# The forward products of decays in a linear-attention kernel: reciprocals of the backward products in place of a second scan

## The chip, the cores and the metric

The kernel runs on one core of a Trainium2 chip. The metric is the device time of one launch in microseconds (us); three runs of the kernel before the change gave 976.2, 979.26 and 980.47 us, a median of 979.26. The engines of the core are TensorE (PE; its weight loads are PEld), VectorE (DVE), ScalarE (ACT), GpSimd (POOL) and SyncE (SP), which issues most of the loads and stores. Each engine works through its own list of instructions in a fixed order and waits on semaphores for the others.

## The reference

Three layers follow each other; the change lies in the first, a recurrence over 768 positions with a state of 40 x 40 for each of 4 batches and 8 heads:

```python
for t in range(S):
    kt, vt, rt = (k[:, :, t], v[:, :, t], r[:, :, t])
    wt, at, bt = (w[:, :, t], a[:, :, t], b[:, :, t])
    y[:, :, t] = np.einsum('bhd,bhde->bhe', rt, state)
    Sa = np.einsum('bhde,bhe->bhd', state, at)
    state_decay = state * wt[:, :, None, :] - np.einsum('bhd,bhe->bhde', Sa, bt)
    state = state_decay + np.einsum('bhd,bhe->bhde', vt, kt)
```

All of it is in fp32. The decays `w` lie between 0.85 and 0.95. The second layer is a gated block (a product, a convolution of three taps, a sigmoid gate, a product), the third adds a two-dimensional Fourier transform, normalizes and runs a two-layer block.

## The kernel before

The recurrence is done in 12 chunks of 64 positions. Within a chunk the effect of the decays is taken out by scaling: `a` is multiplied, and `k` and `b` are divided, by products of decays, so that the rest is made of plain products on TensorE and the inverse of a triangular matrix for each head. A chunk is handled in two halves of two batches, so there are 24 halves, and for each of them `decay` (L153) runs once. Its tiles have 120 partitions (three heads of 40) and six rows of 66 columns: 64 positions with a column of padding at each end. The padding of `w` is zero and that of `ends` is one (column 0 and column 65), so that one scan over 396 columns restarts in each of the six rows.

In `decay`, the first scan (L161) runs backward and gives `vx`: in column 1 + j stands the product of the decays from position j to the end of the chunk. `kb` is multiplied by it on GpSimd (L176). Then a reciprocal of the six entries of column 1 goes into column 0 of `ends` (L164), and a second scan (L165) runs forward from it and gives `wx`: in column j the reciprocal of the product from position j to the end. `a` is multiplied by `wx` (L168; on VectorE in the first chunk, on GpSimd in all others), and goes as a block-diagonal tile `abd` to the products `gram` (L219): by L172 in the first chunk, by three DMAs issued by SP (L175) in the others. `squares` (L247, ScalarE) sums the squares of `wx` and `vx` for a check of the range. Column 65 of `wx` gets a copy of column 1 of `vx` (L166, GpSimd), with which `stage_s` (L458) scales the state; `stage_o` (L509) multiplies the outputs by `wx`.

The order: `run` (L594) writes the first chunks out by hand (with `half`, L632), and then loops over 52 steps, one for each batch of each chunk and a tail of four. A step interleaves the stages of the recurrence, the decays and grams of later chunks (`ahead`, L578: the decay of half (n + 18) / 2 at step n), the inverse of the next group of chunks (L308; many small products on VectorE, L275 and L278 in the first two groups, L333 and L336 in the others), and pieces of preparation for the weights of the later layers (L778 to L785, L752). On top of this a scheduler orders the instructions of each engine when the kernel is built, by its own estimates; TensorE's order is kept as written. `vx` has two buffers, `wx` twelve, `w` and `kb` three. Before the first loads arrive, four products on `ends` (L599) warm TensorE up.

The lines on which all turns:

```python
nc.vector.reciprocal(self.ends.rearrange("p (a b) -> p a b", b=66)[:, :, 0:1], vx[:, :, 1:2])
nc.vector.tensor_tensor_scan(flat[1], flat[0], self.ends, 0.0, op0=ALU.mult, op1=ALU.add)
nc.gpsimd.tensor_copy(wx[:, :, 65:66], vx[:, :, 1:2])
```

Of the kernel before, what the change touches and what calls it, by code (L numbers as in the profile page):

```python
# [15 lines left out]
ALU = mybir.AluOpType  # L16
# [4 lines left out]
C = 64  # L21
# [77 lines left out]
class Attn:  # L99
# [53 lines left out]
    def decay(self, c, hb):  # L153
        nc, pre = self.nc, self.pre
        d = self.hf[c, hb]
        w, a, kb = d["w"], d["a"], d["kb"]

        wx = pre.tile([P3, 6, 66], F32, name="wx", tag="wx", bufs=12)
        vx = self.early.tile([P3, 6, 66], F32, name="vx", tag="vx", bufs=2)
        flat = [v.rearrange("p a b -> p (a b)") for v in (w, wx, vx)]  # L160
        nc.vector.tensor_tensor_scan(flat[2][:, ::-1], flat[0][:, ::-1], self.ends[:, ::-1], 0.0,  # L161
                                     op0=ALU.mult, op1=ALU.add)

        nc.vector.reciprocal(self.ends.rearrange("p (a b) -> p a b", b=66)[:, :, 0:1], vx[:, :, 1:2])  # L164
        nc.vector.tensor_tensor_scan(flat[1], flat[0], self.ends, 0.0, op0=ALU.mult, op1=ALU.add)  # L165
        nc.gpsimd.tensor_copy(wx[:, :, 65:66], vx[:, :, 1:2])  # L166
        e = nc.vector if c < 1 else nc.gpsimd
        e.tensor_tensor(a, a, wx[:, :, 0:C], op=ALU.mult)  # L168
        for h in range(HG):
            if c < 1:  # L170
                mul = nc.vector.tensor_scalar_mul if h == 2 else nc.scalar.mul
                v = mul(self.abd[hb][:, h], a, self.mdiag[:, D * h:D * h + 1])  # L172
                self.late = self.late if h == 2 else v
            else:
                nc.sync.dma_start(self.abd[hb][D * h:D * h + D, h], a[D * h:D * h + D])  # L175
        self.markp = nc.gpsimd.tensor_tensor(kb, kb, vx[:, :, 2:66].unsqueeze(2).to_broadcast([P3, 6, 2, C]), op=ALU.mult)  # L176
        d.update(wx=wx, vx=vx)
# [1232 lines left out]
```

## Time and profile before

| | |
|---|---|
| median of 3 runs | 979.26 us |
| profiled execution | 977.45 us |
| its span | 975.5 us |
| PE busy | 818.7 us (84%) |
| DVE busy | 668.3 us (69%) |
| ACT busy | 519.7 us (53%) |
| POOL busy | 433.2 us (44%) |
| mean granted TensorE clock | 0.925 |

The span is the time from the first to the last instruction of the profiled execution. Busy time is the time in which an engine works on an instruction; waiting is not counted. The recurrence fills the first 480 us, the other two layers the rest. The 24 decays lie between 3.5 us and 341 us.

### The profile page before, as it was taken

To read this page: it belongs to the slowest core of one execution; us is meant where nothing else is said; L and a number is where in the kernel's file an instruction comes from. 1 tells how busy PE (TensorE), PEld (TensorE's weight loads), DVE (VectorE), ACT (ScalarE), POOL (GpSimd) and SP (SyncE) were. 2 spreads that over 40 slices of the span, in tenths; PEclk is the share of its full clock that TensorE was granted. 3 is DMA by queue.
4 is the path that set the end of the run, shared out by engine and by line. 5 is a ranking of instruction groups with operands and counts; after the bars stand their busy time and mean duration, and the time that the engine had idled before them with its cause. 6 is when DMAs were issued, how large, how long until landed. Compare 5 with 4: busy or idle time off the path is not lost. (4 is left out here: it accounts for less than half of the span.)

```text
span 975.5 us, 21804 instructions
## 1 busy us (share of the span) xinstructions
PE 818.7 (84%) x8178; PEld 745.1 (76%) x8178; DVE 668.3 (69%) x1320; ACT 519.7 (53%) x1448; POOL 433.2 (44%) x507
## 2 busy tenths in 40 slices
PE   5457765776886787877899899899999999999997
PEld 3446655676776787776877677777889999999997
DVE  6994897998997898942378688788773544424321
ACT  4747685577676785543566665656553321312211
POOL 5465355465565553532368557665662130101000
PEclk8758797898898999988999999999999999999999
DMA  9623262566564654539444643213004000000001
GB/s 231 187 57 108 80 172 72 167 172 164 162 175 109 172 138 114 159 101 262 121 123 111 208 122 92 79 29 94 14 26 151 22 1 21 21 21 22 21 14 32
DMA packets 102990, 101.16 MB, mean 104 GB/s; under 512 B 47272, under 2 KB 89115, under 8 KB 102875
## 3 DMA queue, kind: packets, MB, share of 16 engines
q1 hardware_dynamic: 100907, 94.73, 34.7%
q0 software_dynamic: 1968, 4.93, 1.7%
q8 instruction: 67, 1.10, 0.5%
q14 instruction: 48, 0.39, 0.1%
HBM read 74.81 MB, written 20.76 MB: 98 GB/s over the span
## 5 line engine op out<-in xcount | busy, mean ns | idle before, releaser
L1132 DVE SCALAR_TENSOR_TENSOR gl<-hp,gh 128x384 fp32r<-128x384 f32 x80 | 44.4, 556 | 111.3 <-ACT gh L1131 111.2
L895 PE MATMUL acc<-w_out_f,z 128*128 128x320 f32 x384 | 116.6, 441 | 3.6 <-POOL z L882 2.1
L1131 ACT ACTIVATE gh<-hp 128x384 fp32r<-128x384 f32 x80 | 39.3, 492 | 149.7 <-PE hp L701 149.6
L878 DVE SCALAR_TENSOR_TENSOR c<-h,cw,c 128x384 f32<-128x384 f32 x128 | 101.6, 798 | 17.3 <-ACT c L876 15.4
L895 PEld LDWEIGHTS acc<-w_out_f,z 128*128 128x128 f32 x384 | 72.1, 193 | 28.2 <-POOL z L882 3.9
L701 PE MATMUL hp<-xh,w_in_h 128*128 128x386 f32 x192 | 76.4, 398 | 12.1 <-ACT h L869 11.9
L701 PE MATMUL hp<-uh,w_ch_h 128*128 128x384 f32 x240 | 82.3, 343 | 0.0
L701 PE MATMUL hp<-ul,w_ch_h 128*128 128x384 f32 x240 | 81.0, 337 | 0.0
L388 PE MATMUL yp<-x,gt 128*64 128x40 f32 x768 | 64.9, 244 | 18.8 <-DVE gt L470 18.4
L1155 POOL DMA_INDIRECT out<-o,rows x12 | 11.8, 982 | 150.8 <-DVE o L1150 131.9
L388 PEld LDWEIGHTS yp<-x,gt 128*64 128x64 f32 x768 | 60.0, 148 | 21.4 <-DVE gt L470 21.4
L219 PE MATMUL gram<-abd,kb 120*128 120x192 f32 (+1 forms) x288 | 59.5, 353 | 17.8 <-DMA a<-in_a 11.2
L1145 PE MATMUL acc<-w_ch_h,gh 128*128 128x320 f32 x240 | 73.2, 312 | 0.0
L1145 PE MATMUL acc<-w_ch_l,gh 128*128 128x320 f32 x240 | 73.0, 309 | 0.0
L333 DVE TENSOR_TENSOR tmp<-A 128x30 f32<-128x30 f32 (+9 forms) x150 | 70.1, 467 | 3.1
L219 PEld LDWEIGHTS gram<-abd,kb 120*128 120x128 f32 x288 | 55.1, 224 | 19.4 <-issue 11.6
L336 DVE TENSOR_TENSOR A<-A,tmp 128x30 f32<-128x30 f32 (+9 forms) x150 | 67.3, 449 | 2.9
L701 PE MATMUL hp<-xl,w_in_h 128*128 128x386 f32 x192 | 67.4, 351 | 0.0
L388 PE MATMUL gp<-rbd,zt 120*128 120x192 f32 (+1 forms) x288 | 59.0, 347 | 7.1 <-ACT zt L437 4.0
L782 POOL TENSOR_TENSOR pm<-pm,py 128x160 int32<-128x160 int32 (+2 forms) x64 | 44.4, 693 | 41.2 <-DVE pm L780 22.3
L879 ACT ACTIVATE c<-c 128x384 f32<-128x384 f32 x64 | 33.4, 521 | 53.9 <-DVE c L878 53.5
L1145 PE MATMUL acc<-w_ch_h,gl 128*128 128x320 f32 x240 | 61.4, 309 | 0.0
(225 smaller groups left out, 2565.0 us busy)
## 6 DMA issues: line engine op xcount, KB each, us to landing
kb<-in_kb SPq DMA_DIRECT2D x24, 360.0 KB
vbd<-in_vbd SPq DMA_DIRECT2D x24, 320.0 KB
xd<-xo SPq DMA_DIRECT2D x56, 90.0 KB
w<-in_w SPq DMA_DIRECT2D x24, 185.6 KB
a<-in_a SPq DMA_DIRECT2D x24, 180.0 KB
z<-in_zv SPq DMA_DIRECT2D x24, 180.0 KB
zt<-in_vt SPq DMA_DIRECT2D x24, 180.0 KB
rbd<-in_r SPq DMA_DIRECT2D x72, 60.0 KB
```

What stands on the lines that cost most here:

```text
L219: nc.tensor.matmul(gp[:, 192 * gi:192 * gi + 64 * nh], d["kb"][:, bl * NG + gi].rearrange("p a b -> p (a b)"), abd[:, 0:nh, bl * NG + gi], ...
L333: nc.vector.tensor_tensor(tmp, A[:, s + 1:32, s:s + 1].to_broadcast([128, n, s]), A[:, s:s + 1, 0:s].to_broadcast([128, n, s]), op=ALU.mult)
L336: nc.vector.tensor_tensor(A[:, s + 1:32, 0:s], A[:, s + 1:32, 0:s], tmp, op=ALU.add)
L388: self.lastpe = op(*args, **kw)
L701: nc.tensor.matmul(out, l, r, start=(j == 0), stop=(j == len(ops) - 1))
L782: nc.gpsimd.tensor_tensor(m, m, y, op=ALU.add)
L878: nc.vector.scalar_tensor_tensor(c, h[:, j:HS + j], cw[:, f, j:j + 1], c, op0=ALU.mult, op1=ALU.add)
L879: nc.scalar.activation(c, c, AF.Sigmoid)
L895: nc.tensor.matmul(self.acc[t][:, 0:DM], z[:, ts], w[:, f], start=(f == 0), stop=(f == NF1 - 1))
L1131: self.mark = nc.scalar.activation(gh, hp[:, 0:HS], AF.Relu)
L1132: nc.vector.scalar_tensor_tensor(gl, hp[:, 0:HS], 0.0, gh.bitcast(F32), op0=ALU.max, op1=ALU.subtract)
L1145: nc.tensor.matmul(self.acc[t][:, 0:DM], l[:, ts], r, start=(f == 0 and j == 0), stop=(f == NF2 - 1 and j == 2))
```

## The change

The small reciprocal into `ends` and the forward scan are replaced by one reciprocal of 6 x 64 elements, from the backward products straight into `wx`. The value is the same product: column j of `wx` is one over column j + 1 of `vx`. Column 64 of `wx`, which the scan wrote and nothing reads, is no longer written. `ends` keeps its first contents.

```diff
-        nc.vector.reciprocal(self.ends.rearrange("p (a b) -> p a b", b=66)[:, :, 0:1], vx[:, :, 1:2])
-        nc.vector.tensor_tensor_scan(flat[1], flat[0], self.ends, 0.0, op0=ALU.mult, op1=ALU.add)
+        nc.vector.reciprocal(wx[:, :, 0:C], vx[:, :, 1:C + 1])
         nc.gpsimd.tensor_copy(wx[:, :, 65:66], vx[:, :, 1:2])
```

The changed kernel has one line less, so its lines behind L164 carry numbers lower by one. TensorE's order is the same in both. VectorE's order at the start of the program, before (a scan is named SCALAR_TENSOR_TENSOR here):

```order
L161 SCALAR_TENSOR_TENSOR vx<-w,ends 120x396
L164 RECIPROCAL ends<-vx 120x6
L165 SCALAR_TENSOR_TENSOR wx<-w,ends 120x396
L161 SCALAR_TENSOR_TENSOR vx<-w,ends 120x396
L168 TENSOR_TENSOR a<-a,wx 120x384
L164 RECIPROCAL ends<-vx 120x6
L172 TENSOR_SCALAR abd_89<-a,mdiag 120x384
L165 SCALAR_TENSOR_TENSOR wx<-w,ends 120x396
L168 TENSOR_TENSOR a<-a,wx 120x384
L172 TENSOR_SCALAR abd_90<-a,mdiag 120x384
```

And VectorE's order at the same place after:

```order
L161 SCALAR_TENSOR_TENSOR vx<-w,ends 120x396
L164 RECIPROCAL wx<-vx 120x6x64
L161 SCALAR_TENSOR_TENSOR vx<-w,ends 120x396
L167 TENSOR_TENSOR a<-a,wx 120x384
L164 RECIPROCAL wx<-vx 120x6x64
L171 TENSOR_SCALAR abd_89<-a,mdiag 120x384
L167 TENSOR_TENSOR a<-a,wx 120x384
L171 TENSOR_SCALAR abd_90<-a,mdiag 120x384
```

The wide reciprocal stands where the small one stood, and the second scan of each decay is gone from between the operations that feed the first grams.

VectorE's order between the two steps of the inverse of the first group, before (L286 gives TensorE the operands of the first products, L300 takes their result):

```order
L286 STREAM_TRANSPOSE t_479<-A 128x32x32
L161 SCALAR_TENSOR_TENSOR vx<-w,ends 120x396
L164 RECIPROCAL ends<-vx 120x6
L165 SCALAR_TENSOR_TENSOR wx<-w,ends 120x396
L161 SCALAR_TENSOR_TENSOR vx<-w,ends 120x396
L313 STREAM_TRANSPOSE A<-l_350 128x1024
L164 RECIPROCAL ends<-vx 120x6
L165 SCALAR_TENSOR_TENSOR wx<-w,ends 120x396
L161 SCALAR_TENSOR_TENSOR vx<-w,ends 120x396
L164 RECIPROCAL ends<-vx 120x6
L165 SCALAR_TENSOR_TENSOR wx<-w,ends 120x396
L270 MEMSET A 128x32
```

And after, at the same place (L299 is the former L300):

```order
L161 SCALAR_TENSOR_TENSOR vx<-w,ends 120x396 x2
L164 RECIPROCAL wx<-vx 120x6x64
L312 STREAM_TRANSPOSE A<-l_348 128x1024
L164 RECIPROCAL wx<-vx 120x6x64
L161 SCALAR_TENSOR_TENSOR vx<-w,ends 120x396
L269 MEMSET A 128x32
L274 TENSOR_TENSOR tmp<-A 128x28
L164 RECIPROCAL wx<-vx 120x6x64
L299 SCALAR_TENSOR_TENSOR t_475<-t_475,mlt,xd 128x16x16
```

Three decays stand ahead of L300 in both; after the change a first product of the next group's inverse stands there too, and the small reciprocals and scans are three wide reciprocals.

## Rows read from the trace of the kernel before

**Rows 1.** Busy time of each engine by stretch of the span; columns in the first line.
```profile
core 0: us, PE busy (x) PEld busy (x) DVE busy (x) ACT busy (x) POOL busy (x), PEclk, DMA share, GB/s
...
10.00:40.00 30.00, 15.26 (x96) 14.81 (x97) 25.60 (x57) 20.44 (x65) 14.44 (x15) 0.72 0.96 253
40.00:75.00 35.00, 17.03 (x437) 15.36 (x435) 33.86 (x55) 19.63 (x64) 19.09 (x20) 0.61 0.20 57
75.00:100.00 25.00, 19.54 (x403) 18.48 (x404) 10.96 (x16) 17.96 (x61) 13.77 (x16) 0.86 0.36 99
100.00:250.00 150.00, 105.04 (x1651) 96.92 (x1651) 133.60 (x263) 102.10 (x323) 79.82 (x85) 0.86 0.50 138
250.00:302.00 52.00, 41.34 (x499) 37.41 (x496) 51.20 (x104) 36.72 (x124) 33.85 (x40) 0.93 0.61 170
302.00:345.00 43.00, 33.19 (x571) 30.91 (x570) 33.81 (x79) 29.61 (x96) 21.80 (x26) 0.84 0.54 143
345.00:480.00 135.00, 111.34 (x1891) 101.74 (x1888) 84.76 (x200) 71.90 (x204) 50.99 (x65) 0.92 0.55 150
```

**Rows 2.** Lines L164, L165 and L1064: duration ns min/median/max, first and last start us.
```profile
L164 DVE RECIPROCAL ends<-vx x24: 160/186/195, 7.0 to 324.1; 120x6 f32<-120x6 f32 x24
...
L165 DVE TENSOR_TENSOR_SCAN wx<-w,ends x24: 968/1098/2389, 7.2 to 339.3; 120x396 f32<-120x396 f32 x24
...
L1064 DVE RECIPROCAL rs<-rs x4: 166/180/191, 707.1 to 883.0; 128x6 f32<-128x6 f32 x4
```

**Rows 3.** Groups of DVE instructions by shape: busy us, mean ns, idle before.
```profile
L165 DVE TENSOR_TENSOR_SCAN wx<-w,ends 120x396 f32<-120x396 f32 x24 | 31.4, 1310 | 0.3
...
L164 DVE RECIPROCAL ends<-vx 120x6 f32<-120x6 f32 x24 | 4.5, 186 | 2.8 <-PE warm L599 2.5
...
L760 DVE COPY cw<-pm 128x24 f32<-128x24 f32 x1 | 0.2, 177 | 0.0
```

**Rows 4.** DVE's timeline from 36 to 45 us: start us, duration us, instruction.
```profile
36.02 0.28 DVE L275 TENSOR_TENSOR tmp<-A 128x112 f32<-128x112 f32 x1
...
39.88 0.19 DVE L275 TENSOR_TENSOR tmp<-A 128x28 f32<-128x28 f32 x1
...
44.91 0.19 DVE L164 RECIPROCAL ends<-vx 120x6 f32<-120x6 f32 x1
```

**Rows 5.** DVE's timeline at the start, with the idle time before in brackets.
```profile
3.53 0.98 DVE L161 TENSOR_TENSOR_SCAN vx<-w,ends 120x396 f32<-120x396 f32 x1 [2.03 <-DMA w<-in_w]
7.01 0.19 DVE L164 RECIPROCAL ends<-vx 120x6 f32<-120x6 f32 x1 [2.49 <-PE warm L599]
```

**Rows 6.** Busy time of line L165 alone, by stretch: length, DVE busy, clock, DMA.
```profile
0.00:75.00 75.00, 13.81 (x9) 0.70 0.59 157
75.00:100.00 25.00, 3.18 (x3) 0.86 0.36 99
100.00:250.00 150.00, 7.87 (x6) 0.86 0.50 138
250.00:302.00 52.00, 4.11 (x4) 0.93 0.61 170
302.00:345.00 43.00, 2.47 (x2) 0.84 0.54 143
```

**Rows 7.** Who waited for whom: us in total, times, longest us.
```profile
ACT w L247 <- DVE wx L165: 44.3, 19, 5.4
...
PE sp L388 <- DVE xo L509: 20.6, 14, 4.3
POOL wx L166 <- DVE wx L165: 18.6, 15, 2.2
...
PE yp L388 <- DVE gt L470: 18.4, 11, 5.1
...
SPq L151 <- DVE wx L165: 15.4, 7, 6.0
```

## The prediction

> **What bounds the kernel now.** I read the page first for the shares: no engine is full over the whole span, so a share over 975.5 us decides nothing here. Next I cut the span into stretches. The line that changes runs 24 times, all before 345 us, so only that part is read closely. In [rows 1] the VectorE (DVE) is busy 25.60 of 30 us in 10 to 40, 33.86 of 35 in 40 to 75, 133.60 of 150 in 100 to 250, and 51.20 of 52 in 250 to 302. TensorE is at 41.34 of 52 in that last stretch, and the other engines are lower. Only in 75 to 100 does DVE rest (10.96 of 25), and after 345 it is at 84.76 of 135 with no decay left to do. So up to 345 us the engine on which the change works is the fullest one. The waits say the same: TensorE waits for DVE's results, 20.6 us in front of `sp` behind `xo` and 18.4 us for `gt` [rows 7]. The table of DMA in 10 to 40 (share 0.96) tells that there the loads are near their limit too [rows 1].
>
> **What is removed.** Per decay a reciprocal of 6 elements (186 ns on average) and the scan that starts from it (1310 ns on average, 31.4 us for 24) go away [rows 3]. The scan alone takes 968 ns when nothing disturbs it; the rest of its mean is disturbance, up to 2389 ns [rows 2]. 24 × (0.186 + 1.310) = 35.9 us of DVE.
>
> A wait goes as well. The old reciprocal writes into `ends`, which the warm-up products read; it stood 2.49 us behind them [rows 5]. The new one writes `wx` and has no reason to wait. And the small copy on GpSimd (L166), which waited 18.6 us in total for the scan [rows 7], writes a part of `wx` that the new operation doesn't touch, and only needs `vx`; the order shows it ahead of the work it used to follow. GpSimd is less full than DVE in every stretch from 10 us to 345 [rows 1], so I give this nothing.
>
> **What is added.** Per decay one reciprocal of 6 × 64 = 384 elements. The trace has none of that width; it has 28 of 6 elements. What one costs per element decides the case. DVE's ordinary operations show a fixed time and about 1.07 ns per element: in the chain of products at 36 to 40 us, 112 elements take 0.28 us and 28 take 0.19 [rows 4], which leaves 0.16 us at no element. A copy of 24 elements, with one input as the reciprocal has, takes 177 ns [rows 3]: 152 ns fixed. A reciprocal of 6 elements should then take about 158 ns. Those that begin on an idle engine take 191 to 195 (the largest of both lines [rows 2]; the 0.19 at 44.91 us is one of them [rows 4]). Some 41 ns of 193 are too much, and there are only six elements to account for them.
>
> Bounds: if all of the 41 ns were paid once per instruction, 384 elements take 193 + 378 × 1.04 = 586 ns. If they are paid per element over six, each takes 41 / 6 = 6.8 ns and the whole 152 + 384 × 6.8 = 2.8 us. If the first result lies in the fixed time and five follow, it is 8.2 ns each and 152 + 383 × 8.2 = 3.3 us (with the 195 of the maximum, 3.45 us). I take 3.3 us. A cost paid once would be an odd one, since a copy and a product, of different kinds, agree on their fixed time within 10 ns.
>
> [...]
>
> So DVE gets 24 × 3.3 − 35.9 = 43.3 us more work.
>
> **Where this lies on the path.** By the stretches of [rows 1], with the scans in each from [rows 6] and 0.186 us for each reciprocal:
> 0 to 75: nine decays, 9 × 3.3 − (13.81 + 1.67) = +14.2 us. DVE idles 5.5 us between 10 and 75, and 2.49 us of wait go at the head; of the rest of this idle time about half is in front of operands that come no earlier. I put +9 on the path. The order shows what is late: between the two transposes and L300 (the second step of the inverse of the first group) stand three reciprocals now as before, and TensorE's next products wait for L300.
> 75 to 100: three decays, +6.2 us, into 14.0 us of idle time. I put +1.
> 100 to 250: six decays, +10.8 us, into 16.4 us of idle time, which doesn't lie where the decays are. Half of it: +5.
> 250 to 302: four decays, +8.3 us, with 0.8 us idle. All: +8.
> 302 to 345: two decays, +3.8 us, into 9.2 us of idle time. +1.5.
> The sum is +24.5 us of 43.3. After 345 nothing catches up, since each engine's order is fixed when the kernel is built. The profiled execution took 977.45 us around its span of 975.5; with 24.5 it is 1002. The median of the runs, 979.26, is 1.8 us above that execution, so I say 1003 us.
>
> **Rivals.**
> One, the excess is paid once and the wide reciprocal takes 0.59 us: faster than before. Then DVE loses 35.9 − 24 × 0.59 = 21.7 us. Head: 2.5 us of wait; the first nine decays 15.5 − 5.3 = 10.2 us, of which half is hidden by the loads of 10 to 40: −5; 250 to 302: 4.9 − 2.4 = −2.5; the other eight between 100 and 345: about 7 us, half on the path: −3.5. Together −13.5, so 964 us. Against it stand only the 41 ns, read from operations of six elements; for it, that nothing wider was ever seen slow. It decides as soon as a wide reciprocal takes under some 1.5 us, since that is what the pair removed costs.
>
> Two, slow but covered. DVE's idle time between 10 and 345 us is 45.9 us by [rows 1], more than the 43.3 us added. If all but the full stretch of 250 to 302 absorbs its part, +8 − 2.5 gives 983 us. Against: most idle times come in pieces in front of TensorE's or GpSimd's results, and these move with DVE.
>
> Three, slow, and nothing is covered: 43.3 − 2.5 gives 1018 us, with 3.45 us each 1022. The mechanism is the queue of loads: SP waits 15.4 us in seven places for `wx` through L165 [rows 7], and ScalarE 44.3 us in 19 for the squares. A `wx` that is late holds loads of later decays and the copies behind the squares, and the lateness is carried on even in stretches with idle time.
>
> Four, the change does nothing: the reciprocal costs about what the pair did (3.5 ns per element, 1.5 us), 977 to 981 us.
>
> **How the numbers follow.** Forecast 0.65 (its own range 990 to 1013: from 2.8 us each with the same share, 24 × 2.8 − 35.9 = 31.3 and 31.3 × 0.57 = 18, to a share of four fifths); one 0.14; two 0.06; three 0.10; four 0.05. What a measurement of this kernel tells from no change is about 0.5%, 4.9 us. Faster gets rival one: 0.15 with a little of four. Slower gets the forecast, three and most of two: 0.78. The rest, 0.07, is the same. The range of 975 to 1022 leaves out rival one and the ends.
>
> **What would show it.** In the profile of the changed kernel the new line has 24 operations of 120x384 with a mean near 3.3 us (80 us in all); 0.6 us makes rival one right and the forecast wrong. DVE's busy time goes from 668.3 to about 710. The first reciprocal begins right behind the first scan, near 4.5 us. The last decay, at 339 us now, comes some 22 us later, and the stretch after 480 us is as long as before. If the line is slow and the last decay no later, two is right; if the shift is over 35 us, three.

## The result, and the profile after

The changed kernel takes 992.72 us (median of 4 runs, 990.79 to 994.83), before it was 979.24 (4 runs): slower by 1.43%, a ratio of 1.0143 with a 95% interval of 1.0114 to 1.0171. Between the two profiled executions the difference is 990.79 − 977.45 = 13.3 us.

First the page's busy times of the kernel after, and the new line's durations (min/median/max in ns, first and last start in us):

```profile
PE 826.3 (84%) x8178; PEld 752.5 (76%) x8178; DVE 692.6 (70%) x1296; ACT 521.5 (53%) x1448; POOL 426.4 (43%) x507
```

```profile
L164 DVE RECIPROCAL wx<-vx x24: 2522/2541/2554, 4.6 to 348.9; 120x384 f32<-120x384 f32 x24
```

One wide reciprocal takes 2.54 us, and 24 of them differ by 32 ns at most. The pair that it replaces took 0.186 + 1.310 us [rows 3]. VectorE's busy time grew by 692.6 − 668.3 = 24.3 us.

VectorE's timeline at the start, after (start us, duration us, idle time before in brackets):

```profile
3.57 0.98 DVE L161 TENSOR_TENSOR_SCAN vx<-w,ends 120x396 f32<-120x396 f32 x1 [2.07 <-DMA w<-in_w]
4.59 2.55 DVE L164 RECIPROCAL wx<-vx 120x384 f32<-120x384 f32 x1
```

The wait of 2.49 us for the warm-up [rows 5] is gone, as forecast. The stretch in which the decays lie, first before:

```profile
core 0: us, PE busy (x) PEld busy (x) DVE busy (x) ACT busy (x) POOL busy (x), PEclk, DMA share, GB/s
10.00:345.00 335.00, 231.41 (x3644) 213.89 (x3644) 289.03 (x570) 226.45 (x727) 182.77 (x199) 0.83 0.52 142
```

And after, with the part of it in which VectorE used to rest, for comparison with [rows 1]:

```profile
10.00:345.00 335.00, 233.43 (x3614) 216.67 (x3614) 301.46 (x526) 222.84 (x710) 168.83 (x190) 0.80 0.52 139
75.00:100.00 25.00, 19.89 (x394) 18.98 (x394) 19.63 (x16) 18.08 (x62) 12.93 (x15) 0.81 0.30 84
```

VectorE's idle time in these 335 us falls from 46.0 to 33.5 us.

Busy times of equal stretches don't say where a delay begins, since the work shifts from one to the next. For that I follow one instruction of each step: ScalarE's copy of the product `u` (L427 before, L426 after, 48 times). Six of the 48 before (steps 0, 8, 15, 16, 17 and 47):

```profile
67.87 0.43 ACT L427 ACTIVATE z<-u 64x320 f32<-64x320 f32 x1 [1.44 <-PE u L388]
...
169.03 0.43 ACT L427 ACTIVATE z<-u 64x320 f32<-64x320 f32 x1
...
230.05 0.43 ACT L427 ACTIVATE z<-u 64x320 f32<-64x320 f32 x1
...
244.06 0.43 ACT L427 ACTIVATE z<-u 64x320 f32<-64x320 f32 x1 [0.39 <-PE u L388]
...
253.50 0.43 ACT L427 ACTIVATE z<-u 64x320 f32<-64x320 f32 x1
...
470.93 0.43 ACT L427 ACTIVATE z<-u 64x320 f32<-64x320 f32 x1 [1.15 <-PE u L388]
```

The same six after:

```profile
67.15 0.43 ACT L426 ACTIVATE z<-u 64x320 f32<-64x320 f32 x1
...
172.14 0.43 ACT L426 ACTIVATE z<-u 64x320 f32<-64x320 f32 x1
...
229.56 0.43 ACT L426 ACTIVATE z<-u 64x320 f32<-64x320 f32 x1
...
252.74 0.43 ACT L426 ACTIVATE z<-u 64x320 f32<-64x320 f32 x1 [0.39 <-PE u L387]
...
267.09 0.43 ACT L426 ACTIVATE z<-u 64x320 f32<-64x320 f32 x1
...
483.78 0.43 ACT L426 ACTIVATE z<-u 64x320 f32<-64x320 f32 x1 [1.81 <-PE u L387]
```

In these two executions the head costs nothing (−0.7 us at step 0, with nine of the 24 decays behind it). At step 8 the copy is 3.1 us late, at step 15 it is early again (−0.5), at step 16 it is 8.7 us late, at step 17 13.6, at the last step 12.9; what follows the recurrence adds 0.5 us. So the time is lost around step 16. Steps 8 and 16 are two of those where a new group's inverse is first used; at the later ones, 24, 32 and 40, the lateness grows only at 32 (from 8.8 to 12.6 us).

VectorE's timeline in front of step 16, after, shows what became late (the last product of the inverse is L335, its transpose L342; `xo` is the output of a step, and TensorE waits for this one too before it comes to the products `bp` of the inverse):

```profile
231.16 0.34 DVE L508 TENSOR_TENSOR xo<-yt,wx 120x192 f32<-120x192 f32 x1
231.43 0.59 DVE L332 TENSOR_TENSOR tmp<-A 128x30 f32<-128x30 f32 x1
231.94 2.54 DVE L164 RECIPROCAL wx<-vx 120x384 f32<-120x384 f32 x1
234.40 0.12 DVE L335 TENSOR_TENSOR A<-A,tmp 128x30 f32<-128x30 f32 x1
...
236.05 1.72 DVE L161 TENSOR_TENSOR_SCAN vx<-w,ends 120x396 f32<-120x396 f32 x1
237.69 0.94 DVE L751 TENSOR_TENSOR wl<-pm,wh 128x256 fp32r<-128x256 f32 x1
238.56 1.94 DVE L342 STREAM_TRANSPOSE t<-A 128x1024 f32<-128x1024 f32 x1
```

TensorE's products behind that transpose, after:

```profile
240.56 3.62 PE L387 MATMUL bp<-t,l 32*32 32x32 f32 x128 [7.27 <-DVE t L342]
```

The same transpose (L343) and the same `xo` (L509) on VectorE before:

```profile
219.61 2.12 DVE L343 STREAM_TRANSPOSE t<-A 128x1024 f32<-128x1024 f32 x1
...
225.16 0.34 DVE L509 TENSOR_TENSOR xo<-yt,wx 120x192 f32<-120x192 f32 x1
...
229.33 0.34 DVE L509 TENSOR_TENSOR xo<-yt,wx 120x192 f32<-120x192 f32 x1
```

And TensorE's products before, with no wait in front of them:

```profile
231.38 2.36 PE L388 MATMUL bp<-t,l 32*32 32x32 f32 x128
```

VectorE has no gap in this stretch after, and TensorE stands still for 7.27 us until the transpose is done. Two things have become different there. The list of VectorE is longer: a reciprocal of 2.54 us stands right ahead of the last product of the inverse. And its order is another: before, the transpose stood ahead of the eleventh and twelfth of the 48 `xo`, after it stands behind the twelfth, since the scheduler ordered the changed program anew. The longer list is the forecast mechanism; the other order is not, and these traces alone don't tell the two apart.

### The profile page after: what moved, and what is told of

It reads as the page before. It is cut to its first block, busy times and chain, and to the rows that moved or that the text cites. A ratio compares the mean times of both kernels' runs of the same rounds, so it can differ in the third digit from the quotient of the medians.

```text
span 988.8 us, 21781 instructions
## 1 busy us (share of the span) xinstructions
PE 826.3 (84%) x8178; PEld 752.5 (76%) x8178; DVE 692.6 (70%) x1296; ACT 521.5 (53%) x1448; POOL 426.4 (43%) x507
## 5 line engine op out<-in xcount | busy, mean ns | idle before, releaser
L700 PE MATMUL hp<-xh,w_in_h 128*128 128x386 f32 x192 | 76.0, 396 | 14.2 <-ACT h L868 13.6
L218 PE MATMUL gram<-abd,kb 120*128 120x192 f32 (+1 forms) x288 | 63.4, 369 | 20.2 <-DVE tmp L274 14.2
L218 PEld LDWEIGHTS gram<-abd,kb 120*128 120x128 f32 x288 | 58.9, 238 | 21.5 <-issue 14.6
L335 DVE TENSOR_TENSOR A<-A,tmp 128x30 f32<-128x30 f32 (+9 forms) x150 | 73.2, 488 | 3.0
L456 POOL TENSOR_TENSOR st<-st,sm 120x360 f32<-120x360 f32 x40 | 39.5, 989 | 68.1 <-DVE sm L455 54.7
L332 DVE TENSOR_TENSOR tmp<-A 128x30 f32<-128x30 f32 (+9 forms) x150 | 65.1, 434 | 3.1
L387 PE MATMUL gp<-rbd,zt 120*128 120x192 f32 (+1 forms) x288 | 61.3, 356 | 6.0 <-ACT zt L436 4.7
```

What stands on the lines that cost most here:

```text
L218: nc.tensor.matmul(gp[:, 192 * gi:192 * gi + 64 * nh], d["kb"][:, bl * NG + gi].rearrange("p a b -> p (a b)"), abd[:, 0:nh, bl * NG + gi], ...
L332: nc.vector.tensor_tensor(tmp, A[:, s + 1:32, s:s + 1].to_broadcast([128, n, s]), A[:, s:s + 1, 0:s].to_broadcast([128, n, s]), op=ALU.mult)
L335: nc.vector.tensor_tensor(A[:, s + 1:32, 0:s], A[:, s + 1:32, 0:s], tmp, op=ALU.add)
L387: self.lastpe = op(*args, **kw)
L456: nc.gpsimd.tensor_tensor(self.st[b], self.st[b], t, op=ALU.add)
L700: nc.tensor.matmul(out, l, r, start=(j == 0), stop=(j == len(ops) - 1))
```

## Experiments

Theory A: time follows VectorE's work for the forward products. Its rival B: the scheduler's other order costs the time. A second question, head or loop, is told apart by using the wide reciprocal in one of them alone. The scheduler orders each of these programs anew, so every edit changes VectorE's order as well, and no run has the changed kernel's order with another duration.

**A cheap operation in its place.** All 24 wide reciprocals become copies:

```diff
-        nc.vector.reciprocal(wx[:, :, 0:C], vx[:, :, 1:C + 1])
+        nc.vector.tensor_copy(wx[:, :, 0:C], vx[:, :, 1:C + 1])
```

> In place of the wide reciprocal stands a copy of the same 384 elements (an estimate of 0.36 us from the fixed 0.15 us and the 0.42 us of the 384-element product with a scalar); the reciprocals are left out. Theory A, the duration on VectorE decides and 0.55 us of time go with each us of its work (13.5 us for 24.3 us): VectorE's work falls by 52 us against the changed kernel, by 27 us against before, so about 964 us. Rival B, the new order of instructions that the scheduler made costs the time, not the duration: near 990 us.

Measured: 971.95 us, ratio to before 0.9932 (0.9905 to 0.9958). Faster than before, so a program with one operation in place of two is not slow for that alone: rival B as I put it falls. (In front of step 16 its transpose stands early in the list, as before, so the place where the changed kernel loses its time is not tried by it.) The gain is half of what A said, and the reason is in the work. VectorE was busy 656.2 us, 12.1 less than before and not 27.

```profile
L164 DVE COPY wx<-vx x24: 348/361/1796, 4.5 to 333.6; 120x384 f32<-120x384 f32 x24
```

**Half the reciprocals.**

```diff
-        nc.vector.reciprocal(wx[:, :, 0:C], vx[:, :, 1:C + 1])
+        nc.vector.reciprocal(wx[:, 0:3, 0:C], vx[:, 0:3, 1:C + 1])
+        nc.vector.tensor_copy(wx[:, 3:6, 0:C], vx[:, 3:6, 1:C + 1])
```

> Three of the six rows get the reciprocal, the other three a copy (their reciprocals are left out): an estimate of 1.35 + 0.3 = 1.65 us per decay, about what the reciprocal and scan of before took (1.50 us). Theory A: 977 to 982 us, as before. Rival B, the order costs the time: 989 to 993 us.

Measured: 983.79 us, ratio 1.0048 (1.0029 to 1.0066). Above A's range by 2 us and below B's by 5, so neither was right. VectorE was busy 666.6 us, 1.7 less than before, and the kernel was slower all the same: busy time alone does not order the runs. The lines also give the price by width:

```profile
L164 DVE RECIPROCAL wx<-vx x24: 1320/1342/1354, 4.4 to 339.4; 120x192 f32<-120x192 f32 x24
L165 DVE COPY wx<-vx x24: 221/228/1532, 5.7 to 340.6; 120x192 f32<-120x192 f32 x24
```

From 192 to 384 elements the median grows by 2541 − 1342 = 1199 ns: 6.24 ns per element, with 143 ns that don't depend on the width.

**Twice.** A second, equal reciprocal behind the first:

```diff
         nc.vector.reciprocal(wx[:, :, 0:C], vx[:, :, 1:C + 1])
+        nc.vector.reciprocal(wx[:, :, 0:C], vx[:, :, 1:C + 1])
```

> The wide reciprocal is issued twice into the same tile: 24 x 2.54 = 61 us more work on VectorE than the changed kernel. Theory A at 0.55: 1026 us; if VectorE has no room left at all, up to 1054 us. Rival B: within 5 us of the changed kernel, 988 to 998 us.

Measured: 1043.37 us, ratio 1.067 (1.0645 to 1.0695). 61 us more work cost 50.7 us of time against the changed kernel, 0.83 per us, between A's two figures. The first 33 us cost about half as much each, and one would think that VectorE's idle time is used up by now. It is not (columns as above):

```profile
10.00:345.00 335.00, 198.57 (x2958) 182.88 (x2958) 300.03 (x475) 191.87 (x610) 145.19 (x164) 0.76 0.43 120
```

VectorE idles 35.0 us here, where it idled 33.5 in the changed kernel; it is TensorE that does less (198.57 us busy, where it was 233.43). From 10 us to the end of the last operation on `wx` VectorE idles 46.0 us before, 33.9 in the changed kernel and 43.7 in this one. Against before this kernel is 25.3 us late at step 4 already, where the changed kernel was not late (−0.9). Why the second reciprocal costs more than the first stays open.

**The head alone, the loop alone.** The wide reciprocal in the first nine halves, and before's pair in the rest (and the reverse, with `>=`), against the changed kernel:

```diff
-        nc.vector.reciprocal(wx[:, :, 0:C], vx[:, :, 1:C + 1])
+        if 2 * c + hb < 9:
+            nc.vector.reciprocal(wx[:, :, 0:C], vx[:, :, 1:C + 1])
+        else:
+            nc.vector.reciprocal(self.ends.rearrange("p (a b) -> p a b", b=66)[:, :, 0:1], vx[:, :, 1:2])
+            nc.vector.tensor_tensor_scan(flat[1], flat[0], self.ends, 0.0, op0=ALU.mult, op1=ALU.add)
```

> The wide reciprocal in the first nine halves only, the reciprocal and scan of before in the other fifteen. Theory A2, the time is lost in the loop behind 100 us, and the head loses nothing (there the scans of before were stretched to 1.5 us on average and a wait of 2.5 us goes): 976 to 980 us. Rival C, the head pays 9 us as predicted: 986 to 990 us.

Measured: 979.54 us, ratio 1.0021 (1.0005 to 1.0037). In the expected range: by the ratio the head pays 2.1 us (0.5 to 3.6), not 9.

> The reverse: the reciprocal and scan of before in the first nine halves, the wide reciprocal in the other fifteen. Theory A2: 990 to 995 us. Rival C: 982 to 986 us.

Measured: 983.24 us, ratio 1.0075 (1.005 to 1.0099). That is neither theory's figure: it lies in the range of rival C, which the run of the head excludes. By the ratio, which counts all six runs where the median is 5.4 us above before, the loop costs 7.3 us (4.9 to 9.7); both parts at once, in the changed kernel, 14.0 (11.2 to 16.7): more than the sum of the two, 9.4, but only just clear of these intervals. Why it should be more stays open. Its trace has much the lateness of the changed kernel's at the group of step 16, +10.4 us against before, and it wins 5 us of this back before step 47 (+5.2), which the changed kernel does not.

**The wait at the head by itself.** The kernel of before, with warm-up products that read another tile:

```diff
-        for _ in range(WARM):
-            nc.tensor.matmul(wm[:, 0:396], self.ends[:, 0:128], self.ends, start=True, stop=True)
+        wv = self.hbd[0].rearrange("p a b c -> p (a b c)")
+        for _ in range(WARM + 1):
+            nc.tensor.matmul(wm[:, 0:320], wv[:, 0:128], wv, start=True, stop=True)
```

> The kernel of before, whose warm-up products read a tile that no decay writes (the zeroed tile of the first batch's state products, 320 columns, five products in place of four): the wait of 2.49 us in front of the first small reciprocal goes, nothing else. If the head's gain of the changed kernel is this wait and is carried to the end: 976.5 to 977.5 us. If it is lost again behind the loads of 10 to 40 us (share 0.96): 979 us, no change.

Measured: 976.45 us, ratio 0.9985 (0.997 to 1.0001). The wait is gone:

```profile
4.67 0.19 DVE L164 RECIPROCAL ends<-vx 120x6 f32<-120x6 f32 x1
4.90 0.98 DVE L165 TENSOR_TENSOR_SCAN wx<-w,ends 120x396 f32<-120x396 f32 x1
```

The median is 1.4 us lower, but the interval just includes no change. The wait is also not all that changed: VectorE's order is another here too, with the transpose in front of step 16 behind the twelfth `xo`, as in the changed kernel. It is the only variant with the whole computation that is not slower than before.

**One operation, the scan.** Before, without the small reciprocal:

```diff
-        nc.vector.reciprocal(self.ends.rearrange("p (a b) -> p a b", b=66)[:, :, 0:1], vx[:, :, 1:2])
         nc.vector.tensor_tensor_scan(flat[1], flat[0], self.ends, 0.0, op0=ALU.mult, op1=ALU.add)
```

> The kernel of before without the small reciprocal: the forward scan starts from the fixed ones, so wx holds plain forward products (the division by the chunk's product is left out). One operation per decay, as in the changed kernel, but the scan. Theory A', time follows VectorE's undisturbed work for the forward products (24 x 0.968 = 23.2 us; the points so far: 8.7 us 972.0, 27.7 us 977.8, 37.6 us 983.8, 61.0 us 992.7): 975 to 977.5 us. Rival B, programs with one operation per decay are ordered worse by some 5 us (the kernel with half of the reciprocals was 5 us slower than before at the same busy time): 981 to 984 us.

Measured: 977.44 us, ratio 0.999 (0.9978 to 1.0003): theory A' (A, with VectorE's work counted as it is when nothing disturbs it) in its range, B out by 4 us. It can't be told from before, so it speaks against B more than for A'.

**Two pieces.**

```diff
-        nc.vector.reciprocal(wx[:, :, 0:C], vx[:, :, 1:C + 1])
+        nc.vector.reciprocal(wx[:, 0:3, 0:C], vx[:, 0:3, 1:C + 1])
+        nc.vector.reciprocal(wx[:, 3:6, 0:C], vx[:, 3:6, 1:C + 1])
```

> The wide reciprocal in two pieces of three rows, nothing left out: 24 x (2 x 1.342 - 2.541) = 3.4 us more work than the changed kernel, another order. Theory A': 993.5 to 996 us. Rival B, the order alone moves the time by 5 us and more: outside 988 to 998 us.

Measured: 990.85 us, ratio 1.0128 (1.0106 to 1.015). That is 2.7 us below the range of A' and inside 988 to 998 us, where B did not put it, so both were wrong. The second piece took 50 ns less than the first, so the added work is 2.2 us and not 3.4:

```profile
L165 DVE RECIPROCAL wx<-vx x24: 1282/1292/1297, 5.8 to 353.9; 120x192 f32<-120x192 f32 x24
```

The median is also 1.9 us below the changed kernel's, with more work, but the two intervals (1.0106 to 1.015, and 1.0114 to 1.0171) overlap, so that difference is not shown. This other order did not move the time by more than 5 us.

**On ScalarE.**

```diff
-        nc.vector.reciprocal(wx[:, :, 0:C], vx[:, :, 1:C + 1])
+        nc.scalar.activation(wx[:, :, 0:C], vx[:, :, 1:C + 1], AF.Ln)
+        nc.scalar.activation(wx[:, :, 0:C], wx[:, :, 0:C], AF.Exp, scale=-1.0)
```

> The reciprocals on ScalarE, as the exponential of minus the logarithm, in two operations of 384 elements. VectorE has no forward work at all: theory A' alone, 969 us. Rival D, ScalarE takes VectorE's place: two operations of about 0.52 us and two loads of its tables of 1.283 us each per decay are 24 x 3.6 = 86 us on an engine that was busy 226 of 335 us between 10 and 345: 990 us or more.

Measured: 995.08 us, ratio 1.0178 (1.0151 to 1.0205). Rival D, in its range: from 10 to 345 us ScalarE becomes the fullest engine (285.25 us, where it was 226; VectorE falls to 238.63). The loads of tables take 59 us in all:

```profile
L164 ACT ACT_TABLE_LOAD x23 | 29.5, 1283 | 1.2 <-PEq L1399 0.8
L165 ACT ACT_TABLE_LOAD x23 | 29.5, 1283 | 0.4
```

```profile
10.00:345.00 335.00, 229.24 (x3478) 212.06 (x3479) 238.63 (x488) 285.25 (x760) 162.85 (x185) 0.78 0.49 133
```

The way to each `wx` is longer here as well, two loads and two operations in a row, and this run doesn't tell it from the fullness of ScalarE.

**The runs as one line.** Take for each kernel the work of its forward products as it is when nothing disturbs it: 24 times the sum of the medians, but for the scan of before, which is disturbed, its least time (0.968 + 0.186 us for the pair; 0.973 for the scan alone is a median). The last column is TensorE's wait for the transpose of the inverse in front of step 16; "early" means that the transpose stands ahead of the eleventh `xo` in VectorE's list, in the others it stands behind the twelfth:

| kernel | work, us | time, us | off the line, us | wait, us |
|---|---|---|---|---|
| copies | 8.7 | 971.95 | +0.9 | 0 (early) |
| scan without seed | 23.4 | 977.44 | +1.0 | 3.89 |
| before (its middle median in the later runs) | 27.7 | 978.2 | +0.2 | 0 (early) |
| before, other warm-up | 27.7 | 976.45 | −1.5 | 1.83 |
| half | 37.7 | 983.79 | +2.2 | 4.79 |
| wide in the head | 40.2 | 979.54 | −3.0 | 0 (early) |
| wide in the loop | 48.5 | 983.24 | −2.3 | 7.26 |
| changed kernel | 61.0 | 992.72 | +2.6 | 7.27 |
| two pieces | 63.2 | 990.85 | −0.1 | 7.85 |

The line is fitted to these nine: 967.9 + 0.36 × work, with a standard error of 0.04 on the slope. None lies more than 3.0 us off it; the kernels were timed in four groups, and the medians of before in these differ by 1.4 us. Twice (122 us) lies 31.1 us above it, so the line does not hold for much more work.

By this line some 12 of the change's 13.5 to 14.5 us are VectorE's work (33.3 × 0.36). That is the most one can put down to it so: fitted without the changed kernel and the two pieces, the slope is 0.29 and the changed kernel comes out at 987.4 us, 5.3 too low. What is left may be the order, or a slope that grows with the work, as the run of twice suggests; these runs don't tell.

The order does set where TensorE waits: with the transpose early there is no wait in front of step 16, with it late there is one, and it is the longer, on the whole, the more work VectorE has (12.07 us in the run of twice). But such a wait alone is not the loss: the scan without seed and before with the other warm-up have it and are not slower than before, and wide in the loop has the changed kernel's wait of 7.3 us and is 9.5 us faster.

TensorE's clock is a rival that no run was made for. The mean granted clock from 10 to 345 us falls from 0.83 to 0.80, and TensorE is busy 826.3 us in all, 7.6 longer. But before with the other warm-up was profiled at 0.909 over its span, lower than the changed kernel's 0.915, with TensorE busy 832.7 us, and took 978.23 us, where before took 977.45 at 0.925. So a lower clock need not cost time in this kernel; that it costs none in the changed kernel is not shown.

## Why the prediction was right, and where not

**What bounds.** Right. VectorE is the engine that decides up to 345 us: less work on it is faster (copies, 971.95 us), more is slower (twice, 1043.37 us), and moved to ScalarE it makes that engine the fullest (285.25 of 335 us) and the kernel slower too (995.08 us).

**The price of the wide reciprocal.** This term of the sum was mis-sized: 3.3 us forecast, 2.54 measured. Of the two readings, 6.8 and 8.2 ns per element, I took the higher, which was an estimate and shown by no row; the measured slope is 6.24 ns with 143 ns fixed. So the choice between the readings was the wrong one; the other gave 2.8 us, inside the range that was kept for it. It is still too much: by the measured line a reciprocal of six elements takes 180 ns, and the prediction read 193 from those on an idle engine, where the median of all 24 was 186 [rows 2]. Some 12 ns too many in six elements are 0.8 us in 384. The kind of mechanism was right: the excess of 41 ns on six elements was a price per element, and rival one (0.59 us, 964 us) is out. With 24 × 2.54 − 35.9 = 25.1 us the sum's first line would have met the 24.3 us by which VectorE's busy time grew.

**The removed pair.** 35.9 us of busy time went, but 24 × (1.310 − 0.968) = 8.2 us of this was disturbance of the scans and not their own work. What that meant is in the last section.

**What lies on the path.** The share of 0.57 held in the sum: 13.3 of 24.3 us is 0.55. That is luck, since the places didn't hold. For the head I put +9 us: with the right price it would have been 22.9 − 15.5 − 2.5 = +5 at most, and it measured −0.7 at step 0, and 2.1 us (0.5 to 3.6) in the run with the wide reciprocal there alone. 75 to 100 took its three reciprocals into idle time, as said (−0.9 us at step 4). From there to step 16 I put +5 and it is +9.4 (from −0.7 to +8.7), all of it between the steps 15, at −0.5 us, and 16; from step 16 to the end it is +4.2 in place of 9.5. Too much at the head and too little around step 16 made up for each other.

The step that failed is that a stretch's own idle time tells what it absorbs. The time was lost in two of 48 steps, at the first step of a group, where TensorE needs the transpose that ends the inverse and that stands at the end of a long chain in VectorE's list; and the scheduler had moved that transpose two outputs further back. The prediction read the order at the start of the program and in front of the first group, and not here. That delays collected along the way fall due at such a place fits steps 8 and 16; at 24 and 40 nothing of the kind is seen.

**The rivals.** Two (slow but covered, 983 us) and three (nothing covered, 1018) both lie outside the measured interval, on either side of it. With the right price they would be 980 and 1000 us and lie outside still, as the right price with the forecast's share (977.45 + 0.57 × 25.1 = 991.8) does not. Four is excluded by the interval.

**The sums.** Two of the prediction's figures are not what its terms give: 979.26 + 24.5 is 1003.8 and not 1003, and the lower end of the forecast's own range, from 2.8 us each, is 977.45 + 18 = 995 and not 990. The measured 992.72 us lies between the two.

**The signs named.** The first reciprocal starts at 4.59 us (said 4.5). VectorE's busy time is 692.6 (said 710) and the last decay starts at 348.9 us, 9.6 later (said 22): both are in the main the over-sized term again. The part after the recurrence is as long as before.

## What to carry to other kernels

A short operation of a kind tells what a wide one will cost only if its time is split into a fixed part and a part per element (here 143 ns and 6.24 ns per element); take the fixed part from another operation of one input (a copy of 24 elements gave an estimate of 152 ns), and keep both ways of counting its elements as a range. On an engine that was busy 289 of 335 us, added work did not cost its own length: about 0.36 of it over nine kernels, and 0.83 where it was doubled again, though the engine still idled 35.0 of these 335 us, where it had idled 33.5. So idle time did not tell here what added work costs; look at which of the engine's results the next engine stands, and whether the scheduler has moved it. One operation in place of two is no gain when it costs 6.2 ns per element and the two together, undisturbed, 2.9.

## What the runs showed of the hardware

The reciprocal on VectorE costs 6.24 ns per element (1342 ns for 192 elements, 2541 for 384; 1292 for 192 right behind another reciprocal), while the scan it replaces costs 968 ns for 396 when undisturbed.

The reciprocals are not disturbed: 2522 to 2554 ns over 24 of them in the changed kernel, 2490 to 2555 in the run with two each. Scans in the same places took 968 to 2389 ns [rows 2], copies of 384 elements 348 to 1796. The trace of before points to GpSimd: nine of its 24 second scans overlap with no instruction of GpSimd and took 968 to 983 ns, the other fifteen do overlap and took 973 to 2389, 1513 on average. All 24 reciprocals of the changed kernel overlap with GpSimd's work. No run here took that work away, so it is not shown to be the cause.

What the scans lost beyond their undisturbed time explains most of VectorE's busy time: by undisturbed work the changed kernel should have 61.0 − 27.7 = 33.3 us more than before and has 24.3; 8.2 us of the difference are the stretching of the second scans, which are gone. The rest of VectorE's work takes about the same (637.4 us before, 634.6 after). It is less in the run with two each (617.7 us) and more with the copies (644.5), but with no forward work on VectorE at all, in the run on ScalarE, it is 631.5: no rule comes out of these.
